# A transform layer on one core: the second inverse stage moved to four quarters of the matrix array

## The chip, the cores and the metric

One NeuronCore of a Trainium2 chip runs the whole program; the other cores are idle. The metric is device time in microseconds (us) of one execution. A profiled execution gives, beside its own time, the span from the first to the last instruction and a trace of every engine: TensorE (PE; its weight loads are shown as PEld), VectorE (DVE), ScalarE (ACT), GpSimd (POOL), and SyncE (SP), which here issues nearly all transfers between HBM and on-chip memory, in one queue in order.

## The reference

The input is x of shape (8, 3136, 256), in float32: 8 batches of 3136 tokens with 256 channels.

```python
def _attn_ref(x, filt_r, filt_i):
    X = np.fft.rfft(x, axis=1)
    Y = X * (filt_r + 1j * filt_i)[None, :, :]
    return np.fft.irfft(Y, n=x.shape[1], axis=1).astype(np.float32)

def _moe_ref(x, w_ch1, w_ch2):            # x is what _attn_ref returns
    mixed = np.real(np.fft.fft(np.fft.fft(x, axis=1), axis=2)).astype(np.float32)
    u = x + mixed
    mu = np.mean(u, axis=-1, keepdims=True)
    var = np.mean((u - mu) ** 2, axis=-1, keepdims=True)
    un = (u - mu) / np.sqrt(var + 1e-06)
    return (u + np.maximum(un @ w_ch1, 0.0) @ w_ch2).astype(np.float32)
```

w_ch1 is 256x1024 and w_ch2 is 1024x256. So a filter along the tokens is applied by a Fourier transform and its inverse, then come a second transform, a normalization of each token and two matrix products.

## The kernel before, in words

All products run on TensorE. To keep float32 accuracy at float16 speed, most operands are split into a high and a low float16 part, and a product is the sum of high x high, high x low and low x high. The first batch (b = 0) uses float32 matmuls in its early stages instead.

The transform along the tokens is done in two stages each way, with a trip through HBM between them: first (d1 in HBM), spectrum, inverse1 (d2 in HBM), inverse2 (dy in HBM). The tokens are then fetched from dy in 49 groups of 256 rows of two tokens each (fetch), the second transform is added and the normalization done (prepare, normalize), and products issues the two matrix products in steps: step q multiplies by a slice of w_ch1 (line 1245, tile h) and two steps later adds the product with a slice of w_ch2 into acc (line 1286).

Every engine's order is fixed while the program is built. Each piece of work is a Python generator that yields the engine it wants, a guessed length and a due time; class Plan plays these through and emits instructions in the order in which its own clock grants them. Rings such as "psf" (four PSUM banks), "ast", "ys" and "b2" (two pages each) stand for buffers that must be free. Due times are counted in steps of products; the constant COME says how many steps ahead of its use a chunk of inverse2 is due (brought), and gate holds work back until a step. On the chip each engine runs its fixed order and waits on semaphores.

The change touches inverse2. It works on a batch in 7 chunks, a chunk in two halves o = 0 and 1 (two columns of j each), and each half fills one PSUM bank y (128 x 512). load_b2 (line 879) brings a chunk from d2 into a page b2: for b > 0 one transfer of 448 KB to 112 partitions, where a partition is one (r, j, l), with l the high or the low part, and each piece is 256 float16 values; for b = 0 two transfers of 224 KB to 56 partitions, a page for each half. The matmuls of b > 0 (line 904) contract over those 112 rows: pass i = 0 with the high table under both parts, pass i = 1 with the low table under the high part and zeros under the low part. Each pass is two matmuls h = 0 and 1 of 64 columns each, which write to the lower and the upper 64 partitions of the bank. So a half takes 4 matmuls, 112 rows x 64 columns, 512 elements along the free direction; the first half of a batch's first chunk uses two tables, so it takes 8 matmuls with 256 elements. For b = 0 (line 900) they are float32 matmuls over 56 rows, one pass, 2 to a half. bring (line 917) copies each bank to ys on ScalarE with a factor, and SP writes ys to dy (lines 930 and 934), for the first two chunks of b = 0 in halves, else once for a chunk.

## Time and profile before

| | |
|---|---|
| median of 3 runs | 1456.27 us (1454.42 to 1456.63) |
| the profiled execution's own time | 1456.11 us |
| its span, first to last instruction | 1454.3 us |
| TensorE matmuls, busy | 1387.6 us, 95% of the span |
| VectorE / ScalarE / GpSimd, busy | 1001.8 / 832.1 / 653.0 us (69% / 57% / 45%) |
| granted TensorE clock, mean | 0.974 of full speed |
| transfers through SP's queue | 267.10 MB, 76.1% of the 16 DMA engines' span |

Busy time of TensorE is the union of its matmuls' times, whose ends are modelled: neighbouring matmuls overlap in the trace, so what one costs is read from the distance between starts.

### The profile page before, as it was taken

To read this page: it belongs to the slowest core of one execution; us is meant where nothing else is said; L and a number is where in the kernel's file an instruction comes from. 1 tells how busy PE (TensorE), PEld (TensorE's weight loads), DVE (VectorE), ACT (ScalarE), POOL (GpSimd) and SP (SyncE) were. 2 spreads that over 40 slices of the span, in tenths; PEclk is the share of its full clock that TensorE was granted. 3 is DMA by queue.
4 is the path that set the end of the run, shared out by engine and by line. 5 is a ranking of instruction groups with operands and counts; after the bars stand their busy time and mean duration, and the time that the engine had idled before them with its cause. 6 is when DMAs were issued, how large, how long until landed. Compare 5 with 4: busy or idle time off the path is not lost.

```text
span 1454.3 us, 30096 instructions
## 1 busy us (share of the span) xinstructions
PE 1387.6 (95%) x11241; PEld 928.5 (64%) x11241; DVE 1001.8 (69%) x2127; ACT 832.1 (57%) x1552; POOL 653.0 (45%) x838
## 2 busy tenths in 40 slices
PE   4658999999999999999999999999999999999998
PEld 1524576667766676667766677666766676666666
DVE  5697676777849785868758676867848786545543
ACT  4377555755757465755666466655666564534341
POOL 2532196138812485228822576227823295322220
PEclk8777999999999999999999999999999999999999
DMA  9967799879975998659985999649895898543430
GB/s 272 255 206 194 197 204 215 229 180 187 202 193 151 245 202 205 184 147 230 241 192 154 204 222 235 171 129 216 194 242 149 196 192 199 141 105 97 104 86 30
DMA packets 400261, 269.03 MB, mean 185 GB/s; under 512 B 217450, under 2 KB 341618, under 8 KB 400114
## 3 DMA queue, kind: packets, MB, share of 16 engines
q1 hardware_dynamic: 400114, 267.10, 76.1%
q8 instruction: 88, 1.44, 0.4%
q14 instruction: 59, 0.48, 0.1%
HBM read 113.41 MB, written 102.76 MB: 149 GB/s over the span
## 4 chain that ended last, share of the span: by engine, by line
PE 73%; DVE 9%; DMA 6%; POOL 4%; ACT 3%; issue 3%; SPq 1%; DVEq 0%; ACTq 0%; POOLq 0%
PE acc L1286 29%; PE h L1245 29%; PE y L904 3%; PE s L589 3%; PE mix L998 2%; DVE pages L1023 2%; DMA x<-x 2%; PE s L698 1%; PE i L835 1%; PE s L699 1%; PE i L837 1%; PE i L836 1%; DVE h L1275 1%; DVE st L1163 1%; DVE x L566 1%
## 5 line engine op out<-in xcount | busy, mean ns | idle before, releaser
L1286 PE MATMUL acc<-w2s,h 128*128 128x256 f16 x4704 | 588.1, 273 | 2.9 <-DVE pages L1300 2.9
L1245 PE MATMUL h<-ut,w1s 128*128 128x512 f16 x2352 | 574.5, 380 | 1.4 <-ACT ut L1204 0.8
L1286 PEld LDWEIGHTS <-h 128*128 128x128 f16 x4704 | 452.8, 98 | 135.4 <-issue 19.4
L1275 DVE SCALAR_TENSOR_TENSOR h<-h,h 128x512 f16<-128x512 f32 x392 | 268.4, 685 | 287.7 <-ACT h L1273 286.8
L1273 ACT ACTIVATE h<-h 128x512 f16<-128x512 f32 x392 | 233.2, 595 | 353.5 <-PE h L1245 343.7
L1245 PEld LDWEIGHTS <-w1s 128*128 128x128 f16 x2352 | 225.3, 98 | 216.3 <-issue 21.5
L1220 POOL TENSOR_TENSOR u<-un,u 128x512 f16<-128x512 f32 x94 | 110.0, 1170 | 306.5 <-ACT u L1214 300.5
L1048 POOL TENSOR_TENSOR pages<-sm,pages 128x508 f32<-128x508 f32 x48 | 61.1, 1274 | 179.5 <-ACT sm L1086 147.3
L1194 ACT ACTIVATE un<-pages,sb 128x256 f32<-128x256 f32 x196 | 108.9, 593 | 20.1 <-DVE sb L1144 15.7
L757 POOL TENSOR_TENSOR y<-yt,y 128x448 f16<-128x448 f32 x98 | 101.0, 1033 | 17.1 <-ACT y L755 16.7
L731 POOL TENSOR_TENSOR yt<-yt,t 128x224 f32<-128x224 f32 x98 | 64.5, 658 | 89.2 <-DVE t L717 88.1
L917 ACT ACTIVATE ys<-y,alpha 128x512 f32<-128x512 f32 x112 | 75.8, 687 | 45.4 <-PE y L904 38.3
L809 POOL TENSOR_TENSOR eo<-ef,eo 128x448 f16<-128x448 f32 x56 | 58.8, 1050 | 95.5 <-ACT eo L806 95.4
L1023 DVE SCALAR_TENSOR_TENSOR pages<-mix,alpha,pages 128x254 f32<-128x254 f32 (+2 forms) x188 | 82.8, 478 | 16.7 <-ACT sm L1086 14.4
L717 DVE SCALAR_TENSOR_TENSOR t<-s,pF,ft 128x448 f32<-128x448 f32 x126 | 83.9, 674 | 9.5 <-PE s L699 9.1
L1163 DVE BATCH_NORM_STATS2 st<-pages 128x6 f32<-128x256 f32 x196 | 80.6, 411 | 10.8 <-POOL pages L1054 9.0
L1300 DVE SCALAR_TENSOR_TENSOR pages<-acc,beta,pages 128x512 f32<-128x512 f32 x98 | 70.0, 743 | 13.7 <-PE acc L1286 13.4
L856 DVE TENSOR_TENSOR bt<-i,bt 112x512 f16<-112x512 f32 x98 | 65.8, 683 | 19.7 <-ACT bt L854 18.9
L717 DVE SCALAR_TENSOR_TENSOR yt<-s,pF,ft 128x448 f32<-128x448 f32 x98 | 66.1, 675 | 13.4 <-PE s L699 13.3
L755 ACT CAST y<-yt 128x448 f16<-128x448 f32 x98 | 55.1, 564 | 34.6 <-POOL yt L733 34.1
L780 POOL TENSOR_TENSOR ef<-yt 128x224 f32<-128x224 f32 x112 | 72.1, 664 | 0.1
L566 DVE SCALAR_TENSOR_TENSOR x<-x,sx,x 112x512 f16<-112x512 f32 x84 | 67.0, 822 | 5.4 <-ACT x L564 5.3
(163 smaller groups left out, 1787.6 us busy)
## 6 DMA issues: line engine op xcount, KB each, us to landing
x<-x SPq DMA_DIRECT2D x56, 448.0 KB
d<-ast SPq DMA_DIRECT2D x112, 224.0 KB
at<-d SPq DMA_DIRECT2D x56, 448.0 KB
d<-bt SPq DMA_DIRECT2D x112, 224.0 KB
out<-pages SPq DMA_DIRECT2D x98, 256.0 KB
pages<-dy SPq DMA_DIRECT2D x92, 256.0 KB
pages<-d SPq DMA_DIRECT2D x49, 448.0 KB
dy<-ys SPq DMA_DIRECT2D x94, 224.0 KB
```

What stands on the lines that cost most here:

```text
L566: nc.vector.scalar_tensor_tensor(x16[:, 1], x, sx[:112, 1:2], x16[:, 0], op0=ALU.mult, op1=ALU.subtract)
L717: nc.vector.scalar_tensor_tensor(out, p, pF[:, 1:2], f, op0=ALU.mult, op1=ALU.mult)
L757: nc.gpsimd.tensor_tensor(y16v[:, 1], yh, y16v[:, 0], op=ALU.subtract)
L917: nc.scalar.activation(ys[:, 2 * o : 2 * o + 2], p, AF.Copy, scale=alphas[b][:, 2:3])
L1023: nc.vector.scalar_tensor_tensor(out, p, al, y, op0=ALU.mult, op1=ALU.add)
L1163: nc.vector.bn_stats(st[:, 2 * t + k], y[:, t, k])
L1194: nc.scalar.activation(un[:, k], y[:, t, k], AF.Identity, bias=sb[:, i, 1:2], scale=sb[:, i, 3:4])
L1220: nc.gpsimd.tensor_tensor(u16[:, :, :, 1], unv, u16[:, :, :, 0], op=ALU.subtract)
L1245: nc.tensor.matmul(p.rearrange("p (t k q) -> p t k q", t=2, k=2), w1s[:, d, hw, 128 * f : 128 * f + 128], utv[:, :, :, d, hx], start=i == ...
L1273: nc.scalar.activation(h[:, 0], p, AF.Relu)
L1275: nc.vector.scalar_tensor_tensor(h[:, 1], p, 0.0, h[:, 0], op0=ALU.max, op1=ALU.subtract)
L1286: nc.tensor.matmul(acc[:, kind], h[:, hh, c0 : c0 + 128], w2s[:, f, hw], start=f == 0 and kind == 0 and i == 0, stop=f == 7 and kind == 1 ...
```

## The change

For b > 0 the high and low part of a piece now lie beside each other along the free direction (b2 is read as p, j, h, l, c) instead of on different partitions, so a half needs 56 rows. The half o = 0 goes to partitions 0 to 55 and o = 1 to 64 to 119, in one page; load_b2 issues two transfers of 224 KB for each chunk, in pieces of 1,024 bytes. The matmuls of a chunk are issued together: three passes (high x high, low x high table, high x low table), in each pass o = 0 and 1, h = 0 and 1: rows 0 to 63 or 64 to 127 of the array by columns 0 to 63 or 64 to 127. Both banks are taken before the first matmul. The tables i2 and i2f stand twice on the partitions. For b = 0 the same order with one float32 pass. In bring, the second half of the first two chunks of b = 0 is copied by VectorE instead of ScalarE, and their dy is written once for a chunk. COME goes from 17 to 18, and the guessed lengths change.

```diff
--- before.py
+++ after.py
@@ -32,9 +32,10 @@
 WIDE = 2
 YBUFS = 5
 FIRST = -15
-COME = 17
+COME = 18
 PIECE = 1.15
 HALF = 1.45
+TWIN = 0.83
 BACKED = 3.8
 FILTERS_ON_ACT = (0, 2, 4, 5, 6, 7)
 RAW_IN = (None, None, "ys", "ys", "ut", "ut", None, None)
@@ -278,20 +279,24 @@
 
     i1f = i1.reshape(28, 112, 2, 28, 2).transpose(1, 0, 3, 2, 4).reshape(112, 28, 112).astype(np.float32)
     i2f = i2.reshape(2, 2, 56, 64).transpose(2, 0, 1, 3).astype(np.float32)
+
+    def both_halves(a):
+        t = np.zeros((128, *a.shape[1:]), a.dtype)
+        t[:56] = t[64:120] = a
+        return t[:120]
+
     s2h, s2l = split16(s2)
     s2h, s2l = s2h.reshape(56, 56, 56), s2l.reshape(56, 56, 56)
     p1 = np.stack([s2h, s2h], axis=2).reshape(56, 112, 56)
     p2 = np.stack([s2l, np.zeros_like(s2l)], axis=2).reshape(56, 112, 56)
-    i2h, i2l = split16(i2.reshape(2, 2, 56, 64))
-    q1 = np.stack([i2h, i2h], axis=3).reshape(2, 2, 112, 64)
-    q2 = np.stack([i2l, np.zeros_like(i2l)], axis=3).reshape(2, 2, 112, 64)
+    i2p = np.stack(split16(i2.reshape(2, 2, 56, 64).transpose(2, 0, 1, 3)), 3)
     return {
         "c_s1f": np.ascontiguousarray(s1.reshape(112, 112).astype(np.float32)),
         "c_s1": np.ascontiguousarray(np.stack(split16(s1.reshape(112, 112)), 1)),
         "c_s2": np.ascontiguousarray(np.stack([p1, p2], 2).transpose(1, 0, 2, 3)),
         "c_i1f": np.ascontiguousarray(i1f),
-        "c_i2f": np.ascontiguousarray(i2f),
-        "c_i2": np.ascontiguousarray(np.stack([q1, q2], 2).transpose(3, 0, 1, 2, 4)),
+        "c_i2f": both_halves(i2f),
+        "c_i2": both_halves(i2p),
         "c_mix": np.ascontiguousarray(cmix.transpose(1, 0, 2)),
     }
 
@@ -349,7 +354,7 @@
     s1f = s1.rearrange("p h u -> p (h u)").bitcast(F32)
     s2 = cp.tile([112, 56, 2, 56], F16, name="s2")
     i1 = cp.tile([112, 28, 2, 112], F16, name="i1")
-    i2 = cp.tile([112, 2, 2, 2, 64], F16, name="i2")
+    i2 = cp.tile([120, 2, 2, 2, 64], F16, name="i2")
     mix = cp.tile([128, 2, 320], F16, name="mix")
     ident = cp.tile([128, 128], F32, name="ident")
     ones = cp.tile([1, 128], F32, name="ones")
@@ -362,14 +367,14 @@
     beta = cp.tile([128, 1], F32, name="beta")
     pages = cp.tile([128, YBUFS + 2, 1024], F32, name="pages")
     i1f = i1.rearrange("p j l u -> p (j l u)").bitcast(F32).rearrange("p (j u) -> p j u", u=112)
-    i2f = cp.tile([56, 2, 2, 64], F32, name="i2f")
+    i2f = cp.tile([120, 2, 2, 64], F32, name="i2f")
 
     def y_page(k):
         return pages[:, k % YBUFS].rearrange("p (t k c) -> p t k c", t=2, k=2)
 
     def b2_page(k, b):
-        page = pages[: 112 if b else 56, YBUFS + k % 2]
-        return (page.bitcast(F16) if b else page).rearrange("p (j h c) -> p j h c", h=2, c=256)
+        page = pages[:120, YBUFS + k % 2]
+        return (page.bitcast(F16) if b else page).rearrange("p (j h l c) -> p j h l c", j=2, h=2, c=256)
 
     def z_page(ch):
         return pages[:112, (ch + YBUFS) % (YBUFS + 2)].rearrange("p (j c) -> p j c", c=256)
@@ -865,80 +870,79 @@
     def load_b2(b):
         yield until(*(("d2", b, ch, h) for ch in range(7) for h in range(2)))
         if b:
-            d2v = d2s[b].rearrange("(m r) j l c -> (r j l) m c", r=2)
+            d2v = d2s[b].rearrange("(m r) j l c -> (r j) m (l c)", r=2)
         else:
             d2v = d2s[b].rearrange("(m r) j c -> (r j) m c", r=2)
         for c in range(7):
             yield gate(brought(b, c) - 3 - (0 if b else 3))
-            for o in range(1 if b else 2):
-                k = yield take("b2")
-                b2 = b2_page(k, b)
-                n = 8 if b else 4
+            k = yield take("b2")
+            b2 = b2_page(k, b)
+            for o in range(2):
                 m = 8 * c + 4 * o
-                yield "SP", 1.95 if b else 1.0, urgent(b, c) - 3
-                nc.sync.dma_start(b2.rearrange("p j h c -> p (j h) c"), d2v[:, m : m + n])
-                b2s[b, c, o] = k, b2
-                done("b2", b, c, o)
+                yield "SP", 1.0, urgent(b, c) - 3
+                nc.sync.dma_start(b2[64 * o : 64 * o + 56].rearrange("p j h l c -> p (j h) (l c)"), d2v[:, m : m + 4])
+            b2s[b, c] = k, b2
+            done("b2", b, c)
 
     def inverse2(b):
         for c in range(7):
             t = urgent(b, c)
             yield gate(brought(b, c) - (0 if b else 3))
-            yield until(("b2", b, c, 0), *((("i2",),) if b == 0 else ()))
+            yield until(("b2", b, c), *((("i2",),) if b == 0 else ()))
             ky = yield take("ys")
             ys = fp.tile([128, 4, 256], F32, tag="ys", name=f"ys_{b}_{c}", bufs=2)
+            k, bt = b2s[b, c]
+            ps = []
             for o in range(2):
-                if b == 0:
-                    yield until(("b2", b, c, o))
-                k, bt = b2s[b, c, o if b == 0 else 0]
                 kp = yield take("psf")
-                p = bank(f"y_{b}_{c}_{o}").rearrange("p (j c) -> p j c", j=2)
-                yield "PE", 0.52 if b else 1.1, t
-                for js, i_ in [(slice(0, 1), 0), (slice(1, 2), 1)] if c == o == 0 else [(slice(0, 2), 1)]:
-                    if b == 0:
-                        for h in range(2):
-                            nc.tensor.matmul(p[64 * h : 64 * h + 64, js], i2f[:, i_, h], bt[:, js, h], start=True, stop=True)
-                        continue
-                    for i in range(2):
+                ps.append((kp, bank(f"y_{b}_{c}_{o}").rearrange("p (j c) -> p j c", j=2)))
+            yield "PE", TWIN if b else 2 * TWIN, t
+            passes = [(0, 0), (1, 0), (0, 1)] if b else [(0, None)]
+            for i, (lx, lw) in enumerate(passes):
+                table = i2[:, :, :, lw] if b else i2f
+                for o in range(2):
+                    row = slice(64 * o, 64 * o + 56)
+                    for js, i_ in [(slice(0, 1), 0), (slice(1, 2), 1)] if c == o == 0 else [(slice(0, 2), 1)]:
                         for h in range(2):
                             nc.tensor.matmul(
-                                p[64 * h : 64 * h + 64, js],
-                                i2[:, i_, h, i],
-                                bt[:, 2 * o + js.start : 2 * o + js.stop, h],
-                                start=i == 0,
-                                stop=i == 1,
+                                ps[o][1][64 * h : 64 * h + 64, js],
+                                table[row, i_, h],
+                                bt[row, js, h, lx],
+                                start=i == 0 and js.start == 0,
+                                stop=i == len(passes) - 1 and js.stop == 2,
                             )
-                if o or b == 0:
-                    give("b2", k)
-                plan.spawn(bring(b, c, o, ys, ky, kp, p), t)
+            give("b2", k)
+            for o in range(2):
+                plan.spawn(bring(b, c, o, ys, ky, *ps[o]), t)
 
     def bring(b, c, o, ys, ky, kp, p):
-        yield "ACT", 0.63
-        nc.scalar.activation(ys[:, 2 * o : 2 * o + 2], p, AF.Copy, scale=alphas[b][:, 2:3])
+        if b == 0 and c < 2 and o:
+            yield "DVE", 0.65
+            nc.vector.tensor_scalar(ys[:, 2 * o : 2 * o + 2], p, alphas[b][:, 2:3], None, op0=ALU.mult)
+        else:
+            yield "ACT", 0.63
+            nc.scalar.activation(ys[:, 2 * o : 2 * o + 2], p, AF.Copy, scale=alphas[b][:, 2:3])
         give("psf", kp)
         done("ys", b, c, o)
         if c == o == 0:
             dys[b] = dp.tile([NS, 2, 256], F32, tag="dy", name=f"dy_{b}", bufs=3)
-        early = b == 0 and c < 2
-        if not (o or early):
+        ysd[b, c] = ysd.get((b, c), 0) + 1
+        if ysd[b, c] < 2:
             return
-        yield until(("ys", b, c, 0))
         rows = dys[b][224 * c : 224 * c + 224].rearrange("(j q) k c -> k q j c", j=4)
-        j0, j1 = (2 * o if early else 0) + (c == o == 0 or c == 0 and not early), 2 * o + 2
         for h in range(2):
-            yield "SP", 0.175 * (j1 - j0)
-            nc.sync.dma_start(rows[h, :, j0:j1], ys[64 * h : 64 * h + 56, j0:j1])
-            if c == 0 and o == (not early):
-                for kind in range(2):
-                    yield "SP", 0.1
-                    nc.sync.dma_start(
-                        rows[kind, 28 * h : 28 * h + 28, 0], ys[64 * h + 28 * kind : 64 * h + 28 * kind + 28, 0]
-                    )
-        if o:
-            give("ys", ky)
-        for i in range(o if early else 0, o + 1):
+            yield "SP", 0.7 - 0.17 * (c == 0)
+            nc.sync.dma_start(rows[h, :, c == 0 :], ys[64 * h : 64 * h + 56, c == 0 :])
+            for kind in range(2 * (c == 0)):
+                yield "SP", 0.1
+                nc.sync.dma_start(
+                    rows[kind, 28 * h : 28 * h + 28, 0], ys[64 * h + 28 * kind : 64 * h + 28 * kind + 28, 0]
+                )
+        give("ys", ky)
+        for i in range(2):
             done("placed", b, c, i)
 
+    ysd = {}
     dys, y_at = {}, {}
 
     def fetch(g):
```

In the program's order for TensorE the 420 float16 matmuls of inverse2 stand in 85 uninterrupted stretches before, and the 630 of the change in 49, one for each chunk.

**TensorE, chunk 2 of batch 2.** y_2_2_0 and y_2_2_1 are the banks of the chunk's two halves, i2 the table, pages holds the b2 page. Before, with the last row of the stretch ahead and the first of the one behind:

```order
L1286 MATMUL acc_11_1_5806<-w2s_93,h16_11_4_5866 128x256
L904 LDWEIGHTS i2_84
L904 MATMUL y_2_2_0_5831<-pages_95,i2_84 64x512
L904 LDWEIGHTS i2_84
L904 MATMUL y_2_2_0_5831<-pages_95,i2_84 64x512
L904 LDWEIGHTS i2_84
L904 MATMUL y_2_2_0_5831<-pages_95,i2_84 64x512
L904 LDWEIGHTS i2_84
L904 MATMUL y_2_2_0_5831<-pages_95,i2_84 64x512
L1245 LDWEIGHTS w1s_92
```

The same place in the change, its first pass and a half:

```order
L1290 MATMUL acc_11_1_5924<-w2s_93,h16_11_3_5946 128x256
L907 LDWEIGHTS i2_84
L907 MATMUL y_2_2_0_5912<-pages_95,i2_84 64x512
L907 LDWEIGHTS i2_84
L907 MATMUL y_2_2_0_5912<-pages_95,i2_84 64x512
L907 LDWEIGHTS i2_84
L907 MATMUL y_2_2_1_5913<-pages_95,i2_84 64x512
L907 LDWEIGHTS i2_84
L907 MATMUL y_2_2_1_5913<-pages_95,i2_84 64x512
L907 LDWEIGHTS i2_84
L907 MATMUL y_2_2_0_5912<-pages_95,i2_84 64x512
L907 LDWEIGHTS i2_84
```

Before, a half's four matmuls stand alone and the other half's come later (with matmuls of h and s1 between); now the twelve of a chunk stand in one stretch, with the bank changing every second matmul.

**TensorE, the first chunks of b = 0.** y_0_c_o are its banks, pt and pb belong to the scaling of the weights, uT is the transposed first token tile that the first product waits for. Before:

```order
L389 MATMUL pt_w1_994<-ident_86,mw1_310 1x128
L900 MATMUL y_0_1_0_1020<-pages_95,i2f_96 64x512 x2
L900 MATMUL y_0_1_1_1031<-pages_95,i2f_96 64x512 x2
L407 MATMUL pb_w1_1040<-row_w1_1005,ones_87 128x2
L900 MATMUL y_0_2_0_1059<-pages_95,i2f_96 64x512 x2
L900 MATMUL y_0_2_1_1070<-pages_95,i2f_96 64x512 x2
L389 MATMUL pt_w2_1073<-ident_86,mw2_449 1x128
L407 MATMUL pb_w2_1099<-row_w2_1082,ones_87 128x2
L900 MATMUL y_0_3_0_1103<-pages_95,i2f_96 64x512 x2
L900 MATMUL y_0_3_1_1115<-pages_95,i2f_96 64x512 x2
L1200 MATMUL uT_0_1155<-ident_86,un_0_0_1148 128x128 x4
```

The change at the same place:

```order
L394 MATMUL pt_w1_995<-ident_86,mw1_310 1x128
L907 MATMUL y_0_1_0_1002<-pages_95,i2f_96 64x512 x2
L907 MATMUL y_0_1_1_1009<-pages_95,i2f_96 64x512 x2
L412 MATMUL pb_w1_1045<-row_w1_1034,ones_87 128x2
L907 MATMUL y_0_2_0_1057<-pages_95,i2f_96 64x512 x2
L907 MATMUL y_0_2_1_1058<-pages_95,i2f_96 64x512 x2
L907 MATMUL y_0_3_0_1077<-pages_95,i2f_96 64x512 x2
L907 MATMUL y_0_3_1_1078<-pages_95,i2f_96 64x512 x2
L394 MATMUL pt_w2_1091<-ident_86,mw2_449 1x128
L907 MATMUL y_0_4_0_1123<-pages_95,i2f_96 64x512 x2
L907 MATMUL y_0_4_1_1124<-pages_95,i2f_96 64x512 x2
L1204 MATMUL uT_0_1154<-ident_86,un_0_0_1138 128x128 x4
```

Chunk 4 now stands ahead of uT; before it stood among the products.

**SP's queue, from the first load of b2 of b = 0 to the first fetch of tokens** (pages<-d2 is the load, dy<-ys the write, pages<-dy the fetch). Before:

```order
L879 DMA pages_95<-d2_0_117 56x4x256 x3
L930 DMA dy_0_996<-ys_0_0_978 56x256
L879 DMA pages_95<-d2_0_117 56x4x256
L934 DMA dy_0_996<-ys_0_0_978 28x256
L930 DMA dy_0_996<-ys_0_0_978 56x2x256
L934 DMA dy_0_996<-ys_0_0_978 28x256
L930 DMA dy_0_996<-ys_0_0_978 56x2x256
L930 DMA dy_0_996<-ys_0_0_978 56x256
L934 DMA dy_0_996<-ys_0_0_978 28x256 x2
L879 DMA pages_95<-d2_0_117 56x4x256
L930 DMA dy_0_996<-ys_0_1_1019 56x2x256 x2
L879 DMA pages_95<-d2_0_117 56x4x256
```

The change, up to the fetch:

```order
L883 DMA pages_95<-d2_0_117 56x4x256 x6
L935 DMA dy_0_1007<-ys_0_0_984 56x3x256
L938 DMA dy_0_1007<-ys_0_0_984 28x256 x2
L935 DMA dy_0_1007<-ys_0_0_984 56x3x256
L938 DMA dy_0_1007<-ys_0_0_984 28x256
L935 DMA dy_0_1007<-ys_0_1_1001 56x4x256
L938 DMA dy_0_1007<-ys_0_0_984 28x256
L935 DMA dy_0_1007<-ys_0_1_1001 56x4x256
L883 DMA pages_95<-d2_0_117 56x4x256 x2
L961 DMA pages_95<-dy_0_1007 128x512 x3
```

Before, two more writes follow the rows shown ahead of the first fetch. With a page for a whole chunk, the loads of three chunks now stand at the head of the queue, and the writes of the first two chunks are 8 instead of 12.

## Rows read from the trace of the kernel before

**Rows 1.** Busy time of each engine before and after 123 us.

```profile
core 0: us, PE busy (x) PEld busy (x) DVE busy (x) ACT busy (x) POOL busy (x), PEclk, DMA share, GB/s
0.00:123.00 123.00, 72.70 (x463) 40.99 (x464) 90.66 (x186) 68.07 (x137) 43.73 (x62) 0.73 0.87 248
123.00:1454.00 1331.00, 1314.87 (x10778) 887.48 (x10777) 911.10 (x1942) 764.07 (x1416) 609.23 (x777) 1.00 0.76 179
```

**Rows 2.** What TensorE waited for: total us, times, longest.

```profile
PE y L900 <- DMA pages<-d: 12.1, 6, 8.9
PE s L698 <- DMA at<-d: 7.1, 3, 6.1
```

**Rows 3.** TensorE's matmuls in order of time, 688 to 700 us: start, us, line, form, count.

```profile
687.84 1.47 PE L1286 MATMUL acc<-w2s,h 128*128 128x256 f16 x12
689.24 0.62 PE L904 MATMUL y<-pages,i 112*64 112x512 f16 x4
689.80 1.47 PE L1245 MATMUL h<-ut,w1s 128*128 128x512 f16 x6
...
692.17 1.48 PE L1286 MATMUL acc<-w2s,h 128*128 128x256 f16 x12
693.49 1.46 PE L1245 MATMUL h<-ut,w1s 128*128 128x512 f16 x6
```

**Rows 4.** The same view, 1050 to 1054 us: a longer stretch of line 904.

```profile
1050.78 1.49 PE L904 MATMUL y<-pages,i 112*64 112x512 f16 x12
1052.20 1.49 PE L1286 MATMUL acc<-w2s,h 128*128 128x256 f16 x12
```

**Rows 5.** Weight loads in order of time, for the stretches of rows 3 and 4.

```profile
689.24 0.14 PEld L904 LDWEIGHTS <-i 112*64 112x64 f16 x4 [0.21 <-issue]
...
1050.78 1.00 PEld L904 LDWEIGHTS <-i 112*64 112x64 f16 x12
```

**Rows 6.** Line 904 alone: count, ns least/median/most, first and last start.

```profile
L904 PEld LDWEIGHTS <-i x420: 106/109/110, 265.2 to 1382.4; 112*64 112x64 f16 x140
L904 PE MATMUL y<-pages,i x420: 269/379/403, 265.2 to 1382.6; 112*64 112x512 f16 x119, 112*64 112x256 f16 x21
```

**Rows 7.** TensorE in order of time, 195 to 203 us: a float32 half.

```profile
196.60 1.47 PE L1286 MATMUL acc<-w2s,h 128*128 128x256 f16 x12
198.00 1.07 PE L900 MATMUL y<-pages,i2f 56*64 56x512 f32 x4
199.01 0.20 PE L698 MATMUL s<-s,at 112*128 112x56 f16 x1
```

**Rows 8.** TensorE in order of time, 84 to 131 us.

```profile
117.06 1.18 PE L1200 MATMUL uT<-ident,un 128*128 128x128 f32 x4 [3.15 <-ACT un L1194]
...
123.16 4.85 PE L1245 MATMUL h<-ut,w1s 128*128 128x512 f16 x11 [0.62 <-DVE ut L1206]
127.94 1.45 PE L900 MATMUL y<-pages,i2f 56*64 56x512 f32 x4
129.32 1.47 PE L1245 MATMUL h<-ut,w1s 128*128 128x512 f16 x6
```

**Rows 9.** The chain that ended last, 84 to 131 us.

```profile
96.23 3.28 DMA pages<-d
...
103.21 5.30 DMA pages<-dy
...
108.53 0.47 DVE keep L1118
```

**Rows 10.** Lines 917 and 879 alone, columns as in rows 6.

```profile
L917 ACT ACTIVATE ys<-y,alpha x112: 667/687/712, 95.1 to 1386.8; 128x512 f32<-128x512 f32 x112
...
L879 SPq DMA_DIRECT2D pages<-d x63: 307/442/1426, 88.1 to 1361.7; - x63
```

**Rows 11.** The page: packets by size, and the DMA engines' busy tenths in 40 slices.

```profile
DMA  9967799879975998659985999649895898543430
...
DMA packets 400261, 269.03 MB, mean 185 GB/s; under 512 B 217450, under 2 KB 341618, under 8 KB 400114
```

## The prediction, made before the changed kernel ran

> **What bounds the kernel now.** I first split the busy times at 123 us, where the first matrix product of the last layer starts [rows 1, 8]. Ahead of that TensorE is busy 73 of 123 us and mostly waits. Behind it, it is busy 1314.9 of 1331 us at the full clock of 2.4 GHz (granted 1.00), while VectorE is busy 911, ScalarE 764 and the DMA engines 76%. So 16 us of TensorE's time are idle there, and the list of its waits [rows 2] has none that repeats: the long ones are loads of the start. From 123 us to the end a microsecond of TensorE's work that goes is a microsecond of the kernel, unless a wait takes its place. Next I read what inverse2 costs in that stream, from starts, since the modelled ends overlap.
>
> **Price of a stretch before.** Twelve acc matmuls followed by a product take 693.49 - 692.17 = 1.32 us from start to start; with a stretch of four y matmuls between them 689.80 - 687.84 = 1.96 us [rows 3]. The stretch costs 0.64 us. A stretch of twelve takes 1.42 us from its first matmul to the next line [rows 4], one of four 0.56 [rows 3], so four more passes (a pass is the pair h = 0, 1) cost 0.86, or 0.215 us each. The pair therefore runs side by side, as 512 elements at 2.4 GHz take 0.213. Two passes are 0.43, and 0.64 - 0.43 = 0.21 us is what entering and leaving the column-halved array costs once per stretch.
>
> There are 98 halves of two passes, 196 passes, in 85 stretches: 196 x 0.215 + 85 x 0.21 = 42.1 + 17.9 = 60.0 us.
>
> **Price after, if four run at once.** 49 chunks of three passes are 147 passes, 147 x 0.215 = 31.6; 49 stretches x 0.21 = 10.3. In the 7 first chunks of a batch the two half-long matmuls of o = 0 stand ahead of o = 1 in the order, so o = 1 ends half a pass late: 7 x 0.11 = 0.8. Together 42.7 us, 17.3 less than before.
>
> That four run at once is what no row shows: the matmuls of before that share the array all start at its first row, and only column halves are seen side by side. The two bounds: all four at once (above), or the two row halves one after the other. Then there are 294 passes, 294 x 0.215 + 10.3 = 73.5 us, 13.5 more than before. I take the first. The row it is nearest to is the pair of column halves [rows 4], which already has two streams of data and two outputs at once without any loss, and o = 0 and o = 1 write to different banks. A page bears on it that no run here shows: the Trainium skill, "TensorE: Matmul & The Clock Gate", Part 3, reports 3.07-fold for four row tiles and 10.6-fold for sixteen. The fixed 0.21 is uncertain as well: the array is now halved in both directions. Between 0.1 and 0.4 us, half and twice the row's value, it moves the sum by -5 to +10 us; I keep 0.21.
>
> **Weight loads.** A pass now needs four loads instead of two, each 0.109 us [rows 6]. In the stretch of twelve, the twelve loads lie within 1.00 us [rows 5] inside 1.42 us, and the passes still follow at 0.215, so loads of the next pass run under the present one. In the stretch of four all loads lie within 0.14 us, so at least several run at once. If the four of a pass ran two by two they would need 0.22 us, just a pass. I price them at nothing; the cover is the running pass. If it were gone, each of the two changes of pass in a chunk would show a load: 2 x 49 x 0.109 = 10.7 us. The Trainium skill, same page, "What overlaps and what doesn't", says that a weight load overlaps a running matmul only when it is for another row group; elsewhere it adds loads into the background buffer. By the first sentence those 10.7 us would be paid. The rows above speak against it, because there all loads are for the same 112 rows as the matmul that runs.
>
> **The float32 batch.** A half costs 199.01 - 196.60 - 1.32 = 1.09 us [rows 3, 7]. Chunks 5 and 6 stand in the full stream in both orders: four halves, 4.4 us, become two stretches, 2.2 if four run at once, -2.2 (in series about 2.0 each, -0.5). Chunk 4 stood among the products, 1.38 us for its first half [rows 8] and 1.09 for its second; it now stands ahead of uT, where TensorE waited 3.15 us for ScalarE [rows 8]. That is -2.5 whatever the quarters do.
>
> **The start.** The chain up to the first product runs through the load of chunk 1's second half (3.28 us), its matmuls, the write to dy and the fetch (5.30) to VectorE's first addition [rows 9]. That load was issued late, at 96.23, because a page held half a chunk and had to come free. Now all four loads of chunks 0 and 1 are issued at once, from the 88.1 us at which the first was [rows 10]; the writes between are 8 instead of 12, at a median issue of about 0.4 us each as for the loads [rows 10]. So the fetch can come 3 to 4 us earlier. But VectorE was busy 91 of 123 us [rows 1], nearly without a break at the end, and gets two copies of about 0.69 us (ScalarE's price [rows 10]). I take -2 us, between 0 and -4.
>
> **Transfers and the rest.** A chunk's load becomes two issues instead of one, 49 more on SP; at 0.44 us that is 22 us of queue time spread over 1,270. Behind each extra issue stand the transposes and stores of the queue; they are planned steps ahead, and TensorE's waits for transfers are single events [rows 2]. The pieces become 1,024 bytes instead of 512: 49 x 896 = 43,904 packets become 21,952, of 400,261 [rows 11], which lightens the DMA engines a little. Copies from the banks stay 112 at 0.69 us, on an engine busy 57%. But a chunk takes two of the four banks at once, and ScalarE frees the second two copies, 1.4 us, after the stretch. The queue order is also another one everywhere. Against 16 us of idle time behind 123 us I put +2 us for new waits, with -4 and +10 as ends (a quarter of the idle time less, or some 60% more).
>
> **Sum.** Against the profiled execution's own 1456.1 us, which is within 0.2 us of the median of the runs: -17.3 - 2.2 - 2.5 - 2 + 2 = -22, so 1434.1 us.
>
> **Rivals.**
> *The row halves run in series.* For: no row shows them at once, and both write to the same 64 partitions of PSUM. Against: column halves double their streams for nothing [rows 4]. Inverse2 then costs +13.5 instead of -17.3, chunks 5 and 6 -0.5 instead of -2.2: 1434.1 + 30.8 + 1.7 = 1466.6 us, slower. It decides from the point where a pass of four takes (60.0 - 10.3 - 0.8) / 147 = 0.33 us: from there on the stage costs more than before. Chance 9%.
> *The loads show at each change of pass*, the rule above: 1434.1 + 10.7 = 1444.8 us. For: four loads in a pass are twice what any row has. Chance 8%.
> *The gain is given back in waits.* The DMA engines are at nine tenths or more in 16 of 40 slices [rows 11], 14 of them behind 123 us. Where transfers set the pace, a faster TensorE only waits for them: 14 of 37 slices of the 20 us saved there is about 8, so 1442 us; with a bank held 1.4 us longer in each tenth chunk or so on top, 1448. For: the saving comes evenly in all stretches. Against: the waits for transfers behind 123 us are few and TensorE is the one that is behind. Chance 11%.
> *Nothing changes*: series in part, with the start's gain against it, within 0.2% (2.9 us). Chance 3%.
> The forecast, four at once with waits about as before, has the rest, 69%, with a range of its own of 1427 to 1441 (start, fixed cost and waits do not all err alike).
>
> **How the numbers follow.** 0.2% is about what a measurement of this kernel tells from no change. Faster is the forecast, the loads and the waits, 88%; the same 3%; slower 9%. The range takes in the loads, the waits and half of the fixed cost's error: 1425 to 1448 us, which leaves out the series and the remote ends of the sum.
>
> **What would show it.** Line 904's successor should have 630 matmuls in 49 stretches; a stretch of twelve should add about 0.86 us to the distance between its neighbours, with four starts close together and then some 0.21 us to the next four. If it adds 1.5, the series is right; if the step between passes is 0.32, the loads. The first product should start near 121 us instead of 123.2. Busy time of TensorE behind it should fall with the span, its idle time stay between 12 and 26 us. Packets should fall by about 22,000. What would make the prediction wrong above all: the quarters do not run side by side, or the two banks taken at once stop spectrum, first and inverse1, which take theirs from the same four.

## The result, and the profile after

The changed kernel takes 1432.68 us (median of 4 runs, 1430.87 to 1435.51) against 1455.35 for the kernel before in the same comparison (4 runs, 1453.48 to 1456.63). The ratio is 0.9847, with a 95% interval of 0.9826 to 0.9868: 1.5% faster, 1.4 us from the forecast of 1434.1. The profiled execution took 1432.25 us, its span 1430.4 instead of 1454.3. One execution of the experiments below (of e8) took 6511.89 us and is left out of its time and its ratio.

The windows of the changed kernel, to be read against [rows 1]:

```profile
0.00:123.00 123.00, 78.02 (x498) 44.10 (x499) 92.61 (x194) 69.76 (x140) 47.99 (x67) 0.76 0.90 258
123.00:1430.00 1307.00, 1287.41 (x10953) 884.57 (x10952) 899.99 (x1936) 761.06 (x1411) 604.68 (x772) 1.00 0.78 182
```

Behind 123 us TensorE's busy time fell by 27.5 us, and the stretch became 24 us shorter: idle time there rose from 16.1 to 19.6 us (1307.00 - 1287.41). TensorE is still the bound. What it waited for, from the list of its waits (us in total, times, longest), against [rows 2]:

```profile
PE y L907 <- DMA pages<-d: 10.7, 3, 8.1
PE s L703 <- DMA at<-d: 9.0, 5, 5.4
...
PE i L840 <- DMA z<-y: 2.1, 2, 1.6
```

Again the long ones are single loads of the start: line 907's three (8.1, 1.6 and 0.9 us) end by 110 us. No wait for a transfer belongs to the new float16 stretches.

**A chunk's stretch.** TensorE's matmuls of the changed kernel in order of time, 284 to 290 us, and the weight loads at the same place, to be read against [rows 3 to 5]:

```profile
284.86 1.47 PE L1290 MATMUL acc<-w2s,h 128*128 128x256 f16 x12
286.26 0.84 PE L907 MATMUL y<-pages,i 56*64 56x512 f16 x12
287.04 1.47 PE L1249 MATMUL h<-ut,w1s 128*128 128x512 f16 x6
```

```profile
286.26 0.36 PEld L907 LDWEIGHTS <-i 56*64 56x64 f16 x12 [0.21 <-issue]
```

From the first acc matmul to the next product are 287.04 - 284.86 = 2.18 us; without a stretch between them they are 1.31 (124.77 to 126.08 in the rows of the start, below). So twelve matmuls, a whole chunk, cost 0.87 us, where one half alone cost 0.64 before. The single starts show how: four matmuls start within 10 ns, the next four 240 ns after them, the last four 216 ns later. Before, a pair of column halves took 0.215 us; now four streams share one such step. All twelve weight loads lie within the first 0.36 us, each pass's ahead of that pass. In the first chunk of a batch the stretch has 18 matmuls and takes 0.780 us, against 0.774 for the others: the half pass that the prediction put there (7 x 0.11 = 0.8 us) does not show.

The float32 batch, 184 to 188 us, against [rows 7]:

```profile
184.83 0.82 PE L1290 MATMUL acc<-w2s,h 128*128 128x256 f16 x6
185.57 1.09 PE L907 MATMUL y<-pages,i2f 56*64 56x512 f32 x8
186.59 1.47 PE L1249 MATMUL h<-ut,w1s 128*128 128x512 f16 x6
```

Eight matmuls, both halves, take 1.02 us from start to next start; before, one half of four took 1.01.

The new line alone (count, ns least/median/most, first and last start), against [rows 6]:

```profile
L907 PEld LDWEIGHTS <-i x630: 102/106/107, 261.3 to 1354.9; 56*64 56x64 f16 x158
L907 PE MATMUL y<-pages,i x630: 269/376/400, 261.3 to 1355.1; 56*64 56x512 f16 x136, 56*64 56x256 f16 x22
```

There are half as many matmuls again, 630 for 420, each as long as before (median 376 ns for 379).

**The start.** TensorE in order of time, 84 to 131 us, against [rows 8]:

```profile
105.21 3.34 PE L907 MATMUL y<-pages,i2f 56*64 56x512 f32 x8 [1.59 <-DMA pages<-d]
...
109.77 3.18 PE L907 MATMUL y<-pages,i2f 56*64 56x512 f32 x8 [0.92 <-DMA pages<-d]
113.45 1.18 PE L1204 MATMUL uT<-ident,un 128*128 128x128 f32 x4 [0.49 <-ACT un L1198]
...
119.28 3.58 PE L1249 MATMUL h<-ut,w1s 128*128 128x512 f16 x12
123.47 1.46 PE L1249 MATMUL h<-ut,w1s 128*128 128x512 f16 x6 [0.62 <-DVE h L1279]
124.77 1.47 PE L1290 MATMUL acc<-w2s,h 128*128 128x256 f16 x12
126.08 1.46 PE L1249 MATMUL h<-ut,w1s 128*128 128x512 f16 x6
```

The kernel before, 129 to 133 us, behind [rows 8]:

```profile
131.42 1.47 PE L1286 MATMUL acc<-w2s,h 128*128 128x256 f16 x12
```

The four matmuls of chunk 4 that stood between products at 127.94 [rows 8] are gone from there, and chunks 3 and 4 stand ahead of uT, which waits 0.49 us instead of 3.15. The first product starts at 119.28 us instead of 121.96, and the first acc matmul at 124.77 instead of 131.42, 6.65 us earlier. Eleven products took 127.94 - 123.16 = 4.78 us before, 0.43 each from start to start; now the twelfth starts 3.2 us behind the first. The granted clock is the larger part of it. Three windows of the kernel before:

```profile
116.00:120.00 4.00, 2.68 (x20) 2.15 (x20) 2.65 (x12) 4.00 (x10) 0.00 (x0) 0.50 1.04 309
120.00:124.00 4.00, 2.61 (x8) 1.11 (x9) 3.90 (x10) 4.00 (x8) 1.55 (x2) 0.50 0.98 245
124.00:128.00 4.00, 4.00 (x12) 1.21 (x11) 3.56 (x7) 1.67 (x4) 3.06 (x4) 0.50 1.03 237
```

and of the changed one:

```profile
116.00:120.00 4.00, 3.81 (x26) 2.92 (x25) 2.83 (x7) 4.00 (x9) 1.63 (x2) 0.50 1.02 265
120.00:124.00 4.00, 3.38 (x14) 1.37 (x14) 3.90 (x10) 3.65 (x7) 3.16 (x5) 0.91 1.03 263
```

Before, TensorE was busy 2.68 of the 4 us ahead of 120 us, and worked at 1.2 GHz (0.50) until 128. Now it was busy 3.81 us there, and from 120.7 us on it had 2.4 GHz (0.91 in the mean of the window).

The loads and the fetch that the prediction's step on the start speaks of (SP, 84 to 104 us), and what TensorE waited for before and within chunk 1:

```profile
86.42 6.61 SPq L883 DMA_DIRECT2D pages<-d  x6
...
102.65 0.37 SPq L961 DMA_DIRECT2D pages<-dy  x1
```

```profile
93.70 0.37 PE L394 MATMUL pt_w<-ident,mw 128*1 128x128 f32 x1 [1.01 <-ACT mw L1384]
94.00 1.97 PE L907 MATMUL y<-pages,i2f 56*64 56x512 f32 x4
96.74 1.97 PE L907 MATMUL y<-pages,i2f 56*64 56x512 f32 x4 [0.76 <-DVE ys L921]
```

The six loads stand together as foreseen. But the last matmul of chunk 0 starts at 91.6 us, and its banks are copied only at 95.94 us (VectorE) and 96.08 (ScalarE), between other work of these engines. Chunk 1 waits 1.01 us behind pt_w, which needs ScalarE's mw, and its second half 0.76 us for the bank that VectorE frees. SP issues its last write at 100.40 us.

Packets, against [rows 11], are 21,345 fewer:

```profile
DMA packets 378916, 269.14 MB, mean 188 GB/s; under 512 B 217983, under 2 KB 320271, under 8 KB 378767
```

### The profile page after: what moved, and what is told of

Read it like the earlier page. It is cut to its first block, busy times and chain, and to the rows that moved or that the text cites. A ratio compares the mean times of both kernels' runs of the same rounds, so it can differ in the third digit from the quotient of the medians.

```text
span 1430.4 us, 30614 instructions
## 1 busy us (share of the span) xinstructions
PE 1365.4 (95%) x11451; PEld 928.7 (65%) x11451; DVE 992.6 (69%) x2129; ACT 830.8 (58%) x1550; POOL 652.7 (46%) x838
## 4 chain that ended last, share of the span: by engine, by line
PE 52%; DVE 3%; DMA 2%; POOL 1%; issue 1%; ACT 1%; SPq 0%; ACTq 0%; POOLq 0%; DVEq 0%
PE acc L1290 21%; PE h L1249 21%; PE s L594 2%; PE y L907 2%; PE mix L1002 1%; DMA at<-d 1%; PE i L840 1%; PE i L842 1%; PE i L841 1%; PE s L703 1%; PE s L704 1%; DVE pages L1027 0%; DMA x<-x 0%; DVE h L1279 0%; DMA z<-y 0%
## 5 line engine op out<-in xcount | busy, mean ns | idle before, releaser
L1198 ACT ACTIVATE un<-pages,sb 128x256 f32<-128x256 f32 x196 | 108.7, 593 | 10.2 <-DVE sb L1148 10.2
L924 ACT ACTIVATE ys<-y,alpha 128x512 f32<-128x512 f32 x110 | 70.3, 683 | 40.0 <-PE y L907 39.8
L722 DVE SCALAR_TENSOR_TENSOR yt<-s,pF,ft 128x448 f32<-128x448 f32 x98 | 66.2, 676 | 21.7 <-PE s L704 20.8
L594 PE MATMUL s<-x,s 112*112 112x512 f16 x252 | 66.5, 382 | 5.4 <-DVE x L571 3.8
```

The source lines that it names most:

```text
L594: nc.tensor.matmul(p, s1[:, hs], x16[:, hx], start=i == 0, stop=i == 2)
L722: nc.vector.scalar_tensor_tensor(out, p, pF[:, 1:2], f, op0=ALU.mult, op1=ALU.mult)
L1198: nc.scalar.activation(un[:, k], y[:, t, k], AF.Identity, bias=sb[:, i, 1:2], scale=sb[:, i, 3:4])
```

## The experiments

Ratios are to the kernel before, run on the same chip beside each group, with 95% intervals. e1 to e4 ran on one chip, e5 to e8 later on the same chip, and e9 to e12 on another; the changed kernel's own comparison is the one above. The planner deals the order anew when a length or a step is changed. In e1 to e4 and e9 neither was: in their traces the engines' order is the changed kernel's except for the lines shown.

**e1. Inside a stretch all of o = 0 first, then o = 1.**

```diff
-            for i, (lx, lw) in enumerate(passes):
-                table = i2[:, :, :, lw] if b else i2f
-                for o in range(2):
-                    row = slice(64 * o, 64 * o + 56)
+            for o in range(2):
+                row = slice(64 * o, 64 * o + 56)
+                for i, (lx, lw) in enumerate(passes):
+                    table = i2[:, :, :, lw] if b else i2f
```

> The changed kernel with the order inside a stretch turned: all passes of o = 0 (rows 0 to 63), then all passes of o = 1 (rows 64 to 127). Every other instruction of every engine stands where it did. Theory (four quarters run at once, and from 123 us on a microsecond of TensorE is a microsecond of the kernel): only the last pass of o = 0 and the first of o = 1 still overlap, so a chunk takes five passes of 0.215 us instead of three: 49 x 0.43 = 21 us more, 1432.7 + 21 = 1454 us, about the time before the change. Rival (the row halves gain nothing by running at once; the gain is from fewer stretches, larger pieces and the start): the order inside a stretch does not matter, 1433 us. Rival (part of TensorE's saving is given back in waits for transfers): less than 14 us more, under 1447 us.

Measured: 1433.13 us, ratio 0.9867 (0.9845 to 0.9889), as the changed kernel. Its matmuls at the same chunk:

```profile
283.13 1.47 PE L1290 MATMUL acc<-w2s,h 128*128 128x256 f16 x12
284.54 0.85 PE L907 MATMUL y<-pages,i 56*64 56x512 f16 x12
285.32 1.47 PE L1249 MATMUL h<-ut,w1s 128*128 128x512 f16 x6
```

The theory that the order makes the halves overlap fell. Six matmuls of o = 0 stand ahead of o = 1 in the program, yet the stretch takes 0.79 us and the starts come in groups of four again: two, 20 ns later two more, then 217 ns to the next pair. The third start carries the wait for the second half's bank: TensorE began o = 1 while four matmuls of o = 0 ahead of it still waited. So this run could not show what halves in series cost; e9 was made for that.

**e9. The later batches read rows 0 to 55 for both halves,** in the same order (o = 1 then computes from o = 0's data; the stage's loads, copies and stores stay).

```diff
-                    row = slice(64 * o, 64 * o + 56)
+                    row = slice(0, 56) if b else slice(64 * o, 64 * o + 56)
```

> The changed kernel, but in the batches after the first o = 1 works on rows 0 to 55 too, with the data and table of o = 0 (so the second half of each chunk comes out as a copy of the first). Every instruction of every engine stands where it did; only the row half differs. Theory (the row halves of the array run at once, and in the run with the halves in turn they still did, because TensorE let the second half's passes start beside the first's): now the halves cannot overlap, a chunk takes six passes of 0.215 us instead of three, 49 x 0.645 = 32 us more, 1464 us. Rival (row halves never overlapped and the gain has another source): 1433 us.

Measured: 1462.56 us, ratio 1.0068 (1.0043 to 1.0093).

```profile
286.12 1.47 PE L1290 MATMUL acc<-w2s,h 128*128 128x256 f16 x12
287.52 1.48 PE L907 MATMUL y<-pages,i 56*64 56x512 f16 x12
288.94 1.47 PE L1249 MATMUL h<-ut,w1s 128*128 128x512 f16 x6
```

The same twelve matmuls now take 1.42 us instead of 0.78, and their starts come in six pairs, 0.240 us apart at first and then 0.216. This is the rival of row halves in series, made real: it costs 49 x 0.64 = 31 us, and the kernel is then slower than before. The row halves of the changed kernel do run at once.

**e2 and e3. One pass less (high data by low table left out), and that pass twice.**

```diff
-            passes = [(0, 0), (1, 0), (0, 1)] if b else [(0, None)]
+            passes = [(0, 0), (1, 0)] if b else [(0, None)]
```

```diff
-            passes = [(0, 0), (1, 0), (0, 1)] if b else [(0, None)]
+            passes = [(0, 0), (1, 0), (0, 1), (0, 1)] if b else [(0, None)]
```

> The changed kernel without the pass with the low part of the table (it leaves out the product of the high part of the data and the low part of the table, in the batches after the first); all else in the same order. Theory (TensorE alone sets the pace): 49 x 0.215 = 10.5 us less, 1422 us. Rival (transfers or the other engines already set the pace in a good part of the stream, so that the saving behind the change is given back): less than half, 1427 us or more.

> The changed kernel with the pass with the low part of the table made twice (the output has that product twice); all else in the same order. Theory (TensorE alone sets the pace): 10.5 us more, 1443 us, the same step as a pass less makes downwards. Rival (there is slack for it in TensorE's 20 us of idle time): less than 6 us more, under 1439 us.

Measured: 1421.01 us (ratio 0.9785, 0.9764 to 0.9806) and 1443.2 us (0.9938, 0.9918 to 0.9958). Against e1 and e4 on the same chip (1433.13 and 1431.91, mean 1432.5) that is -11.5 and +10.7; 49 passes of 0.215 us are 10.5, as the theory had it. A microsecond of TensorE in this stage is a microsecond of the kernel, in both directions.

**e4. Pieces of 512 bytes again.** High and low part on separate halves of the page, and four loads of 112 KB per chunk.

```diff
-        return (page.bitcast(F16) if b else page).rearrange("p (j h l c) -> p j h l c", j=2, h=2, c=256)
+        return (page.bitcast(F16) if b else page).rearrange("p (l j h c) -> p j h l c", j=2, h=2, c=256)
...
-                nc.sync.dma_start(b2[64 * o : 64 * o + 56].rearrange("p j h l c -> p (j h) (l c)"), d2v[:, m : m + 4])
+                for l in range(2 if b else 1):
+                    nc.sync.dma_start(
+                        b2[64 * o : 64 * o + 56, :, :, l].rearrange("p j h c -> p (j h) c"), d2v[:, m : m + 4, l]
+                    )
```

> The changed kernel with the high and low part on different halves of the page, so that a chunk of a later batch is loaded by four transfers of 112 KB in pieces of 512 bytes instead of two of 224 KB in pieces of 1,024: some 22,000 packets and 98 issues more, all other orders the same. Theory (transfers are hidden): within 2 us of 1432.7. Rival (the larger pieces carry part of the gain): 5 us more or worse, 1438 us and up.

Measured: 1431.91 us, ratio 0.985 (0.9822 to 0.9878), with

```profile
DMA packets 402240, 269.15 MB, mean 188 GB/s; under 512 B 219354, under 2 KB 343594, under 8 KB 402090
```

23,324 packets more, and twice the load issues, change nothing that these runs can tell: the 5 us of the rival are not there.

**e5 and e6. Each part alone.** e5 has quarters for the later batches, and the functions of before (loads, matmuls, copies) for b = 0, with COME 17; e6 is the kernel before with the new functions for b = 0 alone.

```diff
+    def load_b2_old(b):
...
+    def inverse2_old(b):
...
+    def bring_old(b, c, o, ys, ky, kp, p):
```

> The later batches as in the change, the first batch's part of the stage (loads by half, one page for a half, two row-wise stretches, copies by ScalarE, dy written by half for two chunks) as before; COME at 17 as before. Theory (the parts add up: later batches about -18 us, chunks 4 to 6 of the first batch -4.7, the start -4.5, new waits +3.5): 1455.4 - 18 + 2 = about 1439 us. Rival (the first batch's part is worth little beyond its matmuls, the start is set by other work): 1434 to 1436 us.

> Only the first batch's part of the change (two transfers into one page, four float32 quarters at once, copies of the first chunks on both engines, dy written once for a chunk); the later batches and COME as before. Theory (the parts add up): chunks 4 to 6 -4.7 and the start -4.5, about 1446 us, with 2 us either way for the other order. Rival (the start is set by other work): -4.7 alone or less, 1450 us and up.

Measured: e5 1449.73 us, ratio 0.9973 (0.9959 to 0.9987); e6 1450.58 us, 0.9982 (0.9969 to 0.9995). e5 missed by 10 us and e6 by more than 4. In e5 the stretches cost as in the changed kernel, and behind 123 us TensorE is busy 17.2 us less than before (1297.7 for 1314.9); but its idle time there is 26.3 us instead of 16.1, so 10.2 us of the gain are given back. The list of its waits has new places:

```profile
PE acc L1371 <- DVE pages L1385: 5.5, 6, 1.9
PE i L844 <- DVE t L726: 4.8, 4, 2.0
...
PE h L1330 <- DMA ut<-u: 4.4, 2, 3.2
```

The parts do not add up: by their ratios 4 and 3 us alone, 22 together. A third thing is at work, and the next runs look for it. e6 has all that the prediction's step on the start names, loads together and 8 writes, and its start gains almost nothing (its fetch is issued at 103.95 us, before at 103.21):

```profile
121.58 0.58 PE L1331 MATMUL h<-ut,w1s 128*128 128x512 f16 x1 [0.61 <-ACT ut L1290]
...
127.74 1.59 PE L989 MATMUL y<-pages,i2f 56*64 56x512 f32 x8
...
130.57 1.47 PE L1372 MATMUL acc<-w2s,h 128*128 128x256 f16 x12
```

With COME at 17 chunk 4 stands among the products again, and the first acc matmul comes 0.85 us earlier than before, not 6.65.

**e7. COME 17 in the changed kernel; e11. COME 18 in the kernel before.**

```diff
-COME = 18
+COME = 17
```

> The changed kernel with COME at 17, as before: chunks of the stage come due one step later. Theory (the loads are early enough either way): the order is dealt anew, within 3 us of 1432.7. Rival (the earlier due time is part of the gain, since a chunk now waits for two loads and two banks): 5 us more or worse.

> The kernel before with COME at 18 alone. Theory (COME only deals the order anew): between 1445 and 1461 us, without a rule for the sign. Rival (an earlier due time is worth 10 us by itself, as the changed kernel loses with 17): 1446 us or less.

Measured: e7 1442.56 us, ratio 0.9935 (0.9919 to 0.995), where the theory had at most 3 us; e11 1461.87 us, 1.0055 (1.0034 to 1.0075), just above the range given. Taking COME back costs the changed kernel 10 us (against e1 and e4 on the same chip), and giving it to the kernel before costs that one 8. So 18 is no better in itself; each number deals another order. In e7 the first acc matmul starts at 127.84 us, 3.1 us later than in the changed kernel. The other 7 lie behind it. The list of waits has new ones, such as

```profile
PE h L1249 <- DMA ut<-u: 5.4, 2, 3.1
...
PE i L840 <- DVE t L722: 2.9, 3, 2.0
```

but idle time is not the larger part. From the first acc matmul on, in the changed kernel and in e7:

```profile
124.77:1430.00 1305.23, 1286.12 (x10948) 883.99 (x10946) 898.22 (x1934) 759.99 (x1409) 602.99 (x771) 1.00 0.77 182
127.84:1440.00 1312.16, 1291.64 (x10948) 885.00 (x10946) 903.16 (x1929) 758.75 (x1407) 603.98 (x768) 0.99 0.77 180
```

The same 10,948 matmuls keep TensorE busy 5.5 us longer, and its idle time is 1.4 us more. One reason is the clock after such waits; e7, around one wait of 1.98 us for VectorE:

```profile
706.00:710.00 4.00, 2.33 (x20) 0.77 (x18) 3.93 (x7) 2.77 (x5) 1.95 (x3) 1.00 1.14 210
711.00:713.00 2.00, 2.00 (x12) 1.86 (x10) 1.04 (x3) 1.93 (x4) 2.00 (x4) 0.50 0.99 256
```

In all, e7 has 13.7 us at 1.2 GHz behind its first acc matmul, the changed kernel 6.8. By estimate, 6.9 us more at half the clock cost 3.4 us; the other 2 us of busy time were not traced.

**e8. All copies from the banks on ScalarE.**

```diff
-        if b == 0 and c < 2 and o:
+        if False:
```

> The changed kernel with the copies of the first two chunks' second halves on ScalarE, as before, instead of VectorE. Theory (the start gains from loads issued together and from fewer writes; VectorE is nearly full there and ScalarE has room): within 1.5 us of 1432.7. Rival (the two copies side by side are what brings the first fetch forward): the first product 1.4 us later, 1434 us or more.

Measured: 1442.42 us (median of five), ratio 0.9931 (0.9916 to 0.9945), where a change within 1.5 us was expected. Two copies cannot cost 10 us; the start shows what did. Its windows and its first products:

```profile
116.00:120.00 4.00, 2.16 (x19) 1.83 (x18) 2.74 (x11) 4.00 (x9) 0.72 (x1) 0.50 1.01 311
120.00:124.00 4.00, 1.77 (x5) 0.81 (x6) 3.90 (x8) 3.97 (x8) 3.72 (x5) 0.50 1.03 263
124.00:128.00 4.00, 3.13 (x8) 1.13 (x8) 2.28 (x6) 0.60 (x1) 0.00 (x0) 0.50 1.02 272
```

```profile
120.36 1.18 PE L1204 MATMUL uT<-ident,un 128*128 128x128 f32 x4 [2.20 <-ACT un L1198]
122.40 0.59 PE L1249 MATMUL h<-ut,w1s 128*128 128x512 f16 x1 [0.85 <-ACT ut L1208]
124.87 5.71 PE L1249 MATMUL h<-ut,w1s 128*128 128x512 f16 x17 [1.88 <-DVE ut L1210]
```

TensorE waits ahead of 120 us, stays at 1.2 GHz past 124, and reaches its first acc matmul at 131.21 us: nearly the whole gain of the start (6.4 of 6.65 us) is gone, and another 5 us go behind it. The rival's fetch is not the reason: it is issued 21.7 us behind the last float32 matmul of inverse1, in the changed kernel 21.6.

**e10. The order of before kept as far as it goes.** The kernel before, with quarters for the later batches: all twelve matmuls at the place of the first half, both banks taken there, the second half's place left empty in the plan.

```diff
+                elif o == 0:
+                    for i, (lx, lw) in enumerate([(0, 0), (1, 0), (0, 1)]):
+                        for q in range(2):
+                            row = slice(64 * q, 64 * q + 56)
...
+                                        i2[row, i_, h, lw],
+                                        bt[row, js, h, lx],
```

> The kernel before, with the quarters in the batches after the first alone: all twelve matmuls at the place of the chunk's first half, the second half's slot kept empty, COME 17, the first batch as before. The planner deals the order anew all the same. Theory (the stage saves 18 us wherever it stands, and each new order adds or takes some 8 us of waits): 1437 us, between 1429 and 1447. Rival (the later batches' quarters are worth only what the run with the first batch as before showed, since the waits follow from the quarters): 1448 us or more.

Measured: 1446.16 us, ratio 0.9957 (0.9936 to 0.9977): at the upper end of what was expected. Taking banks earlier was enough for the planner to deal another order. As in e5, TensorE's busy time behind 123 us falls (by 18.4 us), and its idle time there rises, from 16.1 to 23.6 us.

**e12. Another guess for a chunk's length.**

```diff
-TWIN = 0.83
+TWIN = 0.87
```

> The changed kernel with the planner's guess for a chunk's stretch at 0.87, which is what a stretch adds on the chip, instead of 0.83. Theory (any such number deals the order anew, and the changed kernel has a good deal): 1433 to 1446 us. Rival (a truer guess gives a better order): 1430 us or less.

Measured: 1442.86 us, ratio 0.9922 (0.9894 to 0.9949). The guess that lies nearer the measured 0.87 us gives a slower kernel, with 23.8 us of idle time behind 123 us in the profiled execution, which was the fastest of its five (1437.91 us). No run with another order beat the changed kernel.

## Why the prediction was right

The sum came within 1.4 us of the measured time. Its largest term, the quarters, was right in mechanism and size. That the total fits so well is partly luck: the start gained 3 us more than predicted, by another mechanism, the waits took 1.5 back, and other orders of the same work came out 10 us slower. Between the two profiled executions, from starts, the four terms came out so:

- **Stage of the later batches: -17.3 predicted, -17.8 measured.** 49 stretches take 38.5 us from their first matmul to the next line, and 94 ns of entry each, 43.1 in all (predicted 42.7); 85 took 60.9 (60.0). A stretch costs 0.87 us (0.86 was predicted). The doubt was whether row halves run at once; e9 settles it with everything else held: 31 us for the same matmuls in turn. e2 and e3 show that the time is paid in full. About 10.5 us of the 17.8 are the 49 passes fewer (196 to 147), the other 7 the 36 entries fewer (85 stretches to 49). The fixed price of a stretch stayed about 0.2 us although the array is now halved both ways.
- **Float32 chunks 4 to 6: -4.7 predicted (2.2 and 2.5), about -4.6 measured.** Six halves of 6.4 us became two chunks of 2.0; four entries fewer are the rest.
- **The start: -2 predicted, about -5 between the two executions, of which about -3.6 goes with the changed kernel's order.** The first acc matmul comes 6.65 us earlier; 1.5 of these are chunk 4's first half, counted above. Another 1.55 are there already at the last float32 matmul of inverse1, ahead of inverse2 (82.64 before, 81.09 after); there all kernels shown here differ between 79.6 and 83.0 us, e2 and e9 with the same order by 3 us, so this need not be an effect of the change. The remaining 3.6 lie at the far end of the term's bounds, and not for the reason given. The fetch is issued at 102.65 instead of 103.21, not 3 to 4 us earlier, and counted from that last matmul of inverse1 even 1.0 us later (21.6 for 20.6): the step "so the fetch can come 3 to 4 us earlier" failed. The loads did come together, but late copies and two waits of chunk 1 stood between them and the fetch; how much each of these took was not separated. What came instead was not in the working: TensorE, with chunks 3 and 4 ahead of uT, waits little between 105 and 120 us, gets 2.4 GHz sooner, and the first twelve products need 3.2 us from the first start to the last where they needed 5.4. Of these 2.2 us some 1.5 are the clock (eleven steps of 0.43 us would take 4.7), the rest a wait for VectorE's ut behind the first product [rows 8]. All this hangs on the order: from the last matmul of inverse1 to the first acc matmul it is 48.8 us before, 43.7 in the changed kernel, 43.6 to 43.8 in e1 to e4 and e9, which keep its order, and 45.2 to 49.3 in e5 to e8 and e10 to e12, which do not.
- **New waits: +2 predicted, +3.5 measured** as idle time behind 123 us; that is also what is left of the sum (-17.8 - 4.6 - 5.1 + 3.5 = -24.0, and the spans differ by 23.9).

Of the rivals, series is refuted by e9 and the steps of 216 ns. The weight loads that show at each change of pass are refuted by the same steps: a load of 0.106 us in the open would make them 0.32. "What overlaps and what doesn't" of the Trainium skill's "TensorE: Matmul & The Clock Gate" lets a weight load overlap a running matmul only when it is for another row group. With the loads all in the first 0.36 us, for the same 56 rows as the matmuls that run, this does not hold here. The DMA engines as the bound: e4 speaks against it, and so does the list of waits.

**What the number hides.** The rival of gain given back in waits had 1442 to 1448 us. The changed kernel is not there, but four kernels with the same stage for the later batches are (e7, e8, e10, e12: 1442.4 to 1446.2 us, 0.992 to 0.996), and e5 beyond it. e7, e8 and e12 differ by a planner's number or a copy's engine, worth about nothing by itself; e5 and e10 also lack the quarters of the first batch, some 4.6 us. The stretches of the later batches take about the same in all five, 38.3 to 40.2 us from their first matmul to the next line. So the stage saves some 18 us of TensorE's time wherever it runs, and of the 24 us between the spans about 10 hang on the order that the planner happened to deal, part of it in the start (the first acc matmul is 6.4 us later in e8, 0.7 in e12). The mechanism given for that rival, transfers as the bound, is not what the traces show; there it is single waits for VectorE or for a load, and a low clock, in the start and behind some of the waits.

**What stays open.** Why one number deals a good order and the next a bad one was not found; where the time goes can be read in part from each trace, but no run predicts it. The kernel before may itself be a good or bad deal (e11 is 8 us worse). Quarters with exactly the order of before on every engine were not run, since e10's plan moved. Nor was a kernel of before with both halves of a chunk in one stretch: by the estimate above it would save the 7 us of entries without any quarters.

## What to carry to other kernels

A matmul that uses half the rows and half the columns leaves three quarters of TensorE idle: give the quarters independent products with banks of their own, and price a pass of four as one stream, plus about 0.2 us for each visit. Check it with the same instructions on the same rows (a run that differs in one slice), not by their order in the program. Where a planner sets the order, an edit's price and the new deal come together: try neighbours of its numbers before believing the last 10 us, here 0.7%.

## What the runs showed of the hardware

- **TensorE does not hold to the program's order between row halves.** In e1 six matmuls on rows 0 to 55 stand ahead of six on rows 64 to 119; they start in pairs from either half, and the stretch takes 0.787 us. With both on rows 0 to 55 (e9) it is 1.415. That each engine runs its fixed order, as said ahead of the prediction, holds for TensorE's matmuls within a row half, as far as e1 and e9 show.
- **The granted clock rose sooner where TensorE was busier ahead of the products.** Busy 3.81 of the 4 us ahead of 120 us, it was granted 2.4 GHz from 120.7 us on; busy 2.68 (before) or 2.16 (e8), it stayed at 1.2 GHz to 128.7 us. The changed kernel has chunk 4's float32 matmuls ahead of uT, for another reason, and from 113 us on no wait above 0.49 us up to the first product; the first products had the gain. It fell again inside the stream: in e7 TensorE was busy 2.33 of the 4 us to 710 us, and from 711 to 713 us it had 1.2 GHz.
